# Decay attention with a mixing network: two mask buffers, masks fetched one pair ahead, later stores, fixed tiles

## The chip, the cores and the metric

The kernel runs on one core of a Trainium2 chip. The metric is the time of one execution on the device in microseconds (us), as the median of several runs. The engines are PE (matrix products), PEld (its weight loads), DVE, ACT, POOL (GpSimd) and SP, which issues nearly all DMA transfers. Each engine works through its own list of instructions in order and waits on semaphores for the others; all transfers that SP issues go through one queue.

## The reference

All tensors are fp32; B = 8 batches, H = 8 heads, S = 576 positions, D = 64.

```python
log_f  = np.log(np.clip(f, 0.0001, 1.0))
cum    = np.cumsum(log_f, axis=-1)
decay  = cum[:, :, :, None] - cum[:, :, None, :]
scores = np.where(causal, -1e9, q @ k.T / sqrt(D) + decay)   # causal: above the diagonal
attn   = softmax(scores)                                     # sum + 1e-9
x      = (attn @ v) with the 8 heads side by side            # [8, 576, 512]
h  = x.T @ U @ V                       # rank 32, mixes positions
u  = x + h.T
ch = relu(u @ w_ch1) @ w_ch2           # 512 -> 2048 -> 512
return u + ch
```

The term cum[query] is the same for a whole row of scores, so the softmax does not need it. What the kernel adds to a row of scores is -cum[key], and a very negative number above the diagonal.

## The kernel before

**The sweep.** 32 steps, one for each pair of heads (p = 0 to 31, four pairs a batch); a 33rd finishes the last pair. A step has ten slots, s = 0 to 9, of a few us each. A pair's scores are made in four row blocks of 128 positions (main blocks 0 to 3, the block i being 128(i+1) wide) and a tail of 64 positions; DVE adds the mask and takes each row's maximum (L280, tail L325), ACT exponentiates and sums (L289, L334), PE transposes the weights P in groups into PSUM tiles T (L371), and DVE and ACT copy T into PT (L356, L354). One step later, PE multiplies with the values (tile V, L413 and L415), and the result is transposed back (Tx, L428) and multiplied with the reciprocals rv of the row sums sm (L430). `inverse` makes these: two POOL operations on sm (L347, L348), DVE's reciprocal (L349), a POOL copy (L350).

**The masks.** `load_masks` (L112) builds a pair's mask in SBUF: the DMA L122 reads the row -8 cum of each of the two heads from the DRAM tensor `cumd` and broadcasts it to 128 partitions, in tiles M0 to M3 for the main blocks (128, 256, 384 and 512 KB) and M_t for the tail (two DMAs of 144 KB, L132). POOL then writes the triangle above the diagonal in place with affine_select (L124, L134). There is one buffer for each of these tiles. In step p the masks of pair p+1 are fetched: blocks 3, 1 and 0 at slot 5, block 2 and the tail at slot 7, each DMA when the tile has been read by DVE for pair p. For pair 0 the mask is a memset, and PE adds the decay.

**What else is in a step.** SP also loads q and k (`raw`, L237 to L240) two pairs ahead and v (`vr`, L252, L254) for the pair. ACT rounds q and k to the half qkh, POOL computes the rest qkl (L149, 2.8 us) for the pair after. Behind the 4th pair of each batch comes the mixing, in a step k with k mod 4 = 1 ("mixing steps" 5, 9, 13, 17, 21, 25, 29; Tu, H and `ul`, L498 to L521), which leaves u as two halves uh and ul. They are stored to the DRAM tensor `ud` (L529, L532; 1 MB each), the stores standing on SP ahead of the next step's transfers; I call the steps 10, 14, 18, 22 and 26, which begin with them, ud steps. Then the first 6 of 16 chunks of the network run as a filler of the PE (A, L565; B, L583); `ost` (L597) holds 128 rows of its sum and is stored to `accd` (L598, L602). During the first steps the network's weights are decoded (stg, L72 and L74 on POOL). After the sweep, at about 925 us, the other 10 chunks follow with Winograd-like products (pf, po, px), on weights that the loads `sr` (L800) bring.

**What sets the order.** The lists of PE and SP are in the order in which the Python code runs: each slot's calls, with `run_later` calling what `defer(phase, fn, slots)` has put off by that many slots. The lists of DVE, ACT and POOL are made by the framework's scheduler, which sorts their instructions by its own plan of times, whatever slot they were written in. SBUF for tiles is handed out by pools; a tile can be written when the space's last user is done.

## Time and profile before

| what | value |
|---|---|
| median of 3 runs | 1450.66 us (1448.24 to 1452.08) |
| profiled execution | 1444.87 us |
| its span in the trace | 1443.1 us |
| PE busy | 1224.0 us, 85% of the span |
| DVE, ACT, POOL busy | 842.5, 632.6, 265.1 us |
| instructions | 24194 |
| start of the first step, end of the sweep | 6.7 us, about 925 us |

All rows below are from the one profiled execution, which took 1444.87 us, 5.79 us less than the median. A row of a timeline is an instruction (or a few alike): start, duration, engine, line, operation with its destination and sources, and in brackets how long the engine was idle before it and who ended that. The steps begin where PE issues the scores S_0c: step 10 at 276.8 us, 12 at 340.5, 13 at 364.3, 14 at 393.4, 15 at 424.9, 19 at 535.3, 23 at 650.8, 24 at 675.7, 26 at 734.7, 30 at 851.0. Times "+x" are from the start of the step.

### The profile page before, as it was taken

To read this page: it belongs to the slowest core of one execution; us is meant where nothing else is said; L and a number is where in the kernel's file an instruction comes from. 1 tells how busy PE (TensorE), PEld (TensorE's weight loads), DVE (VectorE), ACT (ScalarE), POOL (GpSimd) and SP (SyncE) were. 2 spreads that over 40 slices of the span, in tenths; PEclk is the share of its full clock that TensorE was granted. 3 is DMA by queue.
4 is the path that set the end of the run, shared out by engine and by line. 5 is a ranking of instruction groups with operands and counts; after the bars stand their busy time and mean duration, and the time that the engine had idled before them with its cause. 6 is when DMAs were issued, how large, how long until landed. Compare 5 with 4: busy or idle time off the path is not lost.

```text
span 1443.1 us, 24194 instructions
## 1 busy us (share of the span) xinstructions
PE 1224.0 (85%) x8465; PEld 1046.7 (73%) x8465; DVE 842.5 (58%) x2151; ACT 632.6 (44%) x1675; POOL 265.1 (18%) x452
## 2 busy tenths in 40 slices
PE   6655798878878788868868877999999999999998
PEld 3432566667666667656656665798889999999998
DVE  4655644534534544534434456998387768767775
ACT  3433444433334343333433443443365555565563
POOL 2444332223223222322232222000000000000000
PEclk8766799999989899989998998999999999999999
DMA  8745564664557366354372643659467475556534
GB/s 232 169 116 116 159 127 74 174 95 97 110 141 145 73 163 121 86 164 115 81 171 66 132 151 105 216 178 310 158 218 250 149 246 192 179 186 226 167 115 121
DMA packets 152842, 219.82 MB, mean 152 GB/s; under 512 B 18000, under 2 KB 86096, under 8 KB 150672
## 3 DMA queue, kind: packets, MB, share of 16 engines
q1 hardware_dynamic: 152448, 218.01, 55.4%
q8 instruction: 67, 1.10, 0.3%
q14 instruction: 55, 0.45, 0.1%
q10 hardware_dynamic: 272, 0.26, 0.1%
HBM read 170.89 MB, written 47.33 MB: 151 GB/s over the span
## 4 chain that ended last, share of the span: by engine, by line
PE 53%; DMA 19%; DVE 5%; SPq 4%; POOL 4%; ACT 3%; issue 3%; POOLq 0%; DVEq 0%; ACTq 0%
PE pf L1083 13%; DMA M<-cumd 11%; PE po L1175 7%; PE A L565 5%; PE B L583 5%; PE px L1175 3%; DMA M_t<-cumd 3%; PE T L371 3%; PE V L413 3%; POOL qkl L149 2%; PE Hb L906 2%; PE O L922 2%; DMA ud<-ul 2%; PE pf L1175 2%; ACT P L289 2%
## 5 line engine op out<-in xcount | busy, mean ns | idle before, releaser
L371 PE MATMUL T<-ident,P 128*128 128x128 f32 x640 | 118.4, 315 | 95.1 <-DVE PT L356 86.5
L371 PEld LDWEIGHTS T<-ident,P 128*128 128x128 f32 x640 | 89.2, 163 | 117.1 <-issue 86.5
L1306 ACT COPY mc<-pf 128x512 f32<-128x512 f32 x139 | 81.6, 587 | 169.1 <-PE pf L1083 169.1
L124 POOL TENSOR_SCALAR_AFFINE_SELECT M<-M 128x256 f32<-128x256 f32 x128 | 53.4, 417 | 437.7 <-DMA M<-cumd 359.1
L565 PE MATMUL A<-uh,w1h 128*128 128x256 f32 (+1 forms) x384 | 124.0, 323 | 2.1 <-DVE hl L569 2.1
L413 PE MATMUL V<-PT,vr 128*64 128x448 f32 (+3 forms) x640 | 101.5, 459 | 26.5 <-ACT PT L354 20.9
L565 PE MATMUL A<-ul,w1h 128*128 128x256 f32 (+1 forms) x384 | 117.3, 305 | 0.0
L565 PE MATMUL A<-uh,w1l 128*128 128x256 f32 (+1 forms) x384 | 117.1, 305 | 0.0
L356 DVE COPY PT<-T 128x256 f32<-128x256 f32 (+1 forms) x192 | 73.8, 415 | 52.2 <-PE T L371 51.7
L413 PEld LDWEIGHTS V<-PT,vr 128*64 128x64 f32 x640 | 43.0, 145 | 81.1 <-issue 37.7
L1234 POOL TENSOR_TENSOR xn<-xn,xn 128x512 f32<-128x512 f32 x1 | 1.3, 1270 | 529.9 <-DMA out_dram<-xn 529.9
L583 PE MATMUL B<-w2h,hh 128*128 128x512 f32 x216 | 94.7, 438 | 3.3 <-DVE ost L597 3.3
L349 DVE RECIPROCAL rv<-sm 128x9 f32<-128x9 f32 x32 | 6.9, 214 | 144.1 <-POOL sm L348 144.1
L583 PE MATMUL B<-w2l,hh 128*128 128x512 f32 x216 | 88.3, 409 | 0.0
L583 PE MATMUL B<-w2h,hl 128*128 128x512 f32 x216 | 87.9, 407 | 0.0
L565 PEld LDWEIGHTS A<-uh,w1h 128*128 128x128 f32 x384 | 76.9, 200 | 2.8 <-DVE hl L569 2.3
L569 DVE SCALAR_TENSOR_TENSOR hl<-A,hh 128x256 fp32r<-128x256 f32 (+1 forms) x96 | 43.3, 452 | 59.0 <-ACT hh L573 59.0
L565 PEld LDWEIGHTS A<-uh,w1l 128*128 128x128 f32 x384 | 76.9, 200 | 0.1
L565 PEld LDWEIGHTS A<-ul,w1h 128*128 128x128 f32 x384 | 76.5, 199 | 0.2 <-DVE ul L503 0.2
L149 POOL TENSOR_TENSOR qkl<-raw,qkh 128x1216 fp32r<-128x1216 f32 x26 | 72.4, 2783 | 15.2 <-ACT qkh L146 14.2
L1083 PE MATMUL pf<-d,b1h 128*128 128x256 f32 x320 | 69.5, 280 | 0.0
L446 ACT CAST xh<-xn 128x640 fp32r<-128x640 f32 x32 | 23.2, 726 | 102.7 <-DVE xn L395 102.7
(321 smaller groups left out, 3909.7 us busy)
## 6 DMA issues: line engine op xcount, KB each, us to landing
un<-ud SPq DMA_DIRECT2D x16, 1024.0 KB, 6.4
M<-cumd SPq DMA_DIRECT2D x31, 512.0 KB, 5.7
d<-ud SPq DMA_DIRECT2D x48, 256.0 KB, 4.2
M<-cumd SPq DMA_DIRECT2D x31, 384.0 KB, 5.9
twd<-xn SPq DMA_DIRECT2D x40, 256.0 KB, 2.9
raw<-in_qk_dram SPq DMA_DIRECT2D x32, 288.0 KB, 8.2
Th<-twd SPq DMA_DIRECT2D x35, 256.0 KB, 3.7
tw<-twd SPq DMA_DIRECT2D x35, 256.0 KB, 2.9
```

Of the source, the lines that this page charges most:

```text
L124: nc.gpsimd.affine_select(d, d, [[0, 2], [-1, P]], ALU.is_ge, MASKED, base=0, channel_multiplier=1)
L149: leng.tensor_tensor(dl, src, dh.bitcast(F32), op=ALU.subtract)
L289: nc.scalar.activation(pt, ps, AF.Exp, bias=z["nm"][:, col : col + 1], scale=-1.0, accum_out=z["sm"][:, col : col + 1])
L356: defer(2, lambda: nc.vector.tensor_copy(dst, src))
L371: nc.tensor.transpose(tp[:, P * (x + c) : P * (x + c) + P], z["P"][j][i][:, P * c : P * c + P], ident)
L413: nc.tensor.matmul(ps, vr[:, c, j], pt[:, j, c, lo:hi], start=c == 0, stop=lo == 0)
L565: nc.tensor.matmul(ps[:, :nt], wt[:, fc, c], ut[:, c, sl], start=m == 0, stop=m == 3 * NDC - 1)
L569: nc.vector.scalar_tensor_tensor(hl[:, fc, :nt], ps[:, :nt], 0.0, hh.bitcast(F32)[:, fc, :nt], op0=ALU.max, op1=ALU.subtract)
L583: nc.tensor.matmul(ps, ht[:, fc, P * x : P * x + P], wt[:, fc], start=fc == 0 and m == 0, stop=fc == NA - 1 and m == 2,)
L1083: nc.tensor.matmul(ps, a[x][:, c], b[y][:, c], start=start and m == 0, stop=m == 5, skip_group_check=True)
L1175: nc.tensor.matmul(ps[:, HT * x : HT * x + HT], f[a][:, P * x : P * x + P], w[b], start=k.i == 0 and m == 0 and x == 0 and not (k.n == NG ...
L1306: nc.scalar.copy(mc, FA)
```

## The change

Masks get two buffers (pool `sb2` for `sb`). In step p the masks of pair p+2 are fetched, all five tiles at slot 5, ahead of q and k in the code. The triangles become a function of their own, `triangles`, called for pair p+1 at slot 4 (blocks 3, 1, 0) and at slot 7 (block 2 and tail). The masks of pair 1 are fetched at the start, right behind the store of `cumd`. The `ud` stores are put off by 5 slots for 2, the `accd` stores by 3 slots where they followed at once. The tiles for v are two fixed ones whose empty half is zeroed once, so one of three DMAs for each pair goes; the tile PT4 is one fixed tile, zeroed once, so the memset L365 in each step goes.

```diff
--- before.py
+++ after.py
@@ -104,35 +104,46 @@
     nc.vector.memset(warm, 1.0)
     for raw in RAW:
         nc.vector.memset(raw[:, QT:KO], 0.0)
+    VR = [att.tile([P, NM + 1, P], F32, name=f"vr{x}") for x in range(2)]
+    for vr in VR:
+        nc.gpsimd.memset(vr[64:128, NM], 0.0)
+    PT4 = att.tile([P, P], F32, name="PT4")
+    nc.gpsimd.memset(PT4[64:128], 0.0)
     ident = cst.tile([P, P], F32, name="ident")
     make_identity(nc, ident)
     xn = [cst.tile([P, NM + 1, DM], F32, name=f"xn{i}") for i in range(NX)]
 
-    def load_masks(p, mains):
+    def load_masks(p):
         if p >= NP:
             return
-        z = st[p]
-        for i in (3, 1, 0) if mains == 0 else (2,):
+        z = st.setdefault(p, {"M": {}})
+        for i in (3, 1, 0, 2):
             w = P * (i + 1)
-            m = z["M"][i] = sb.tile([P, 2, w], F32, tag=f"M{i}", name=f"M{p}_{i}")
+            m = z["M"][i] = sb2.tile([P, 2, w], F32, tag=f"M{i}", name=f"M{p}_{i}")
             if p == 0:
                 nc.gpsimd.memset(m, 0.0)
             else:
                 src = cumd.rearrange("(j p) s -> p j s", j=2)[p, :, 0:w]
                 nc.sync.dma_start(m, src.unsqueeze(0).broadcast_to([P, 2, w]))
-            d = m[:, :, P * i : w]
-            nc.gpsimd.affine_select(d, d, [[0, 2], [-1, P]], ALU.is_ge, MASKED, base=0, channel_multiplier=1)
-        if mains == 0:
-            return
-        m = z["M"][NM] = sb.tile([P, S], F32, tag="Mt", name=f"M{p}_t")
+        m = z["M"][NM] = sb2.tile([P, S], F32, tag="Mt", name=f"M{p}_t")
         if p == 0:
             nc.gpsimd.memset(m, 0.0)
+            return
         for j in range(2):
-            if p:
-                nc.sync.dma_start(m[OWN[j]], cumd[j * B * NHP + p].unsqueeze(0).broadcast_to([64, S]))
-            d = m[OWN[j], MAIN:S]
-            nc.gpsimd.affine_select(d, d, [[-1, TAIL]], ALU.is_ge, MASKED, base=0, channel_multiplier=1)
-
+            nc.sync.dma_start(m[OWN[j]], cumd[j * B * NHP + p].unsqueeze(0).broadcast_to([64, S]))
+
+    def triangles(p, rows):
+        if p >= NP:
+            return
+        for i in rows:
+            m = st[p]["M"][i]
+            if i < NM:
+                d = m[:, :, P * i : P * i + P]
+                nc.gpsimd.affine_select(d, d, [[0, 2], [-1, P]], ALU.is_ge, MASKED, base=0, channel_multiplier=1)
+                continue
+            for j in range(2):
+                d = m[OWN[j], MAIN:S]
+                nc.gpsimd.affine_select(d, d, [[-1, TAIL]], ALU.is_ge, MASKED, base=0, channel_multiplier=1)
 
     w1h = wt.tile([P, NA, NDC, P], F32R, name="w1h")
     w1l = wt.tile([P, NA, NDC, P], F32R, name="w1l")
@@ -233,7 +244,7 @@
             return
         b, hp = divmod(p, NHP)
         raw = RAW[p % 2]
-        st[p] = {"b": b, "hp": hp, "raw": raw, "M": {}}
+        st.setdefault(p, {"M": {}}).update(b=b, hp=hp, raw=raw)
         nc.sync.dma_start(raw[:, KO:QW], qk[p, :, 1])
         nc.sync.dma_start(raw[:, 0:MAIN], qk[p, :, 0, 0:MAIN])
         for j in range(2):
@@ -247,11 +258,10 @@
 
     def load_v(p):
 
-        vr = sb2.tile([P, NM + 1, P], F32, tag="vr", name=f"vr{p}")
+        vr = VR[p % 2]
         st[p]["vr"] = vr.rearrange("p c (j d) -> p c j d", j=2)
         nc.sync.dma_start(vr[:, 0:NM], v[p, 0:MAIN].rearrange("(c p) d -> p c d", p=P))
-        for r in range(2):
-            nc.sync.dma_start(vr[64 * r : 64 * r + 64, NM], v[p, MAIN:S])
+        nc.sync.dma_start(vr[0:64, NM], v[p, MAIN:S])
 
     def terms(p):
         z = st[p]
@@ -361,8 +371,6 @@
         z = st[p]
         if "PT" not in z:
             z["PT"] = sb.tile([P, 2, NM, S], F32, tag="PT", name=f"PT{p}")
-            z["PT4"] = sb.tile([P, P], F32, tag="PT4", name=f"PT4{p}")
-            nc.gpsimd.memset(z["PT4"][64:128], 0.0)
         tp = psT.tile([P, 512], F32, tag="T", name=f"T{p}_{j}{g}")
         x = 0
         for i in GRP[g]:
@@ -383,8 +391,7 @@
     def turn_keys(p):
         tq = psT.tile([P, 512], F32, tag="T", name=f"Ty{p}")
         nc.tensor.transpose(tq[0:64, 0:P], st[p]["ptl"][:, MAIN:S], ident)
-        pt4 = st[p]["PT4"]
-        defer(0, lambda: nc.scalar.copy(pt4[0:64], tq[0:64, 0:P]))
+        defer(0, lambda: nc.scalar.copy(PT4[0:64], tq[0:64, 0:P]))
 
     def turn_last(p):
         z = st[p]
@@ -413,7 +420,7 @@
                 nc.tensor.matmul(ps, vr[:, c, j], pt[:, j, c, lo:hi], start=c == 0, stop=lo == 0)
         for j in range(2):
             nc.tensor.matmul(
-                rest[OWN[j], MAIN - P : S - P], vr[:, NM, j], z["PT4"][:, 64 * j : 64 * j + 64], start=False, stop=True
+                rest[OWN[j], MAIN - P : S - P], vr[:, NM, j], PT4[:, 64 * j : 64 * j + 64], start=False, stop=True
             )
         defer(1, lambda: nc.vector.tensor_copy(xT[:, 0:P], head[:, 0:P]))
         defer(1, lambda: nc.vector.tensor_copy(xT[:, P:S], rest[:, 0 : S - P]))
@@ -531,7 +538,7 @@
                         jt = b // 2
                         nc.sync.dma_start(ud[B, :, x, :, P * jt : P * jt + P], t.bitcast(F32)[:, :, MAIN : MAIN + P])
 
-            defer(4, use, 2)
+            defer(4, use, 5)
 
         h = [(0.43, lambda i=i: hmix(i)) for i in range(NM + 1)]
         t = [(0.43, lambda i=i: tu(i)) for i in range(NM)] + [(0.25, tv)]
@@ -595,11 +602,11 @@
                     ost = sf2.tile([P, DM], F32, tag="ost", name=f"ost{b}_{ci}")
                     if ci < NM:
                         nc.vector.tensor_tensor(ost, ps, X[:, ci], op=ALU.add)
-                        nc.sync.dma_start(accd[b, ci], ost)
+                        defer(5, lambda: nc.sync.dma_start(accd[b, ci], ost), 3)
                     else:
                         nc.vector.tensor_tensor(ost[0:64], ps[0:64], X[0:64, NM], op=ALU.add)
                         nc.vector.tensor_tensor(ost[64:128], ps[64:128], xn[(b - 1) % NX][0:64, NM], op=ALU.add)
-                        nc.sync.dma_start(accd[B, b // 2], ost)
+                        defer(5, lambda: nc.sync.dma_start(accd[B, b // 2], ost), 3)
 
                 defer(1, use)
 
@@ -639,13 +646,14 @@
         ):
             own = ident[rows, col : col + 1]
             nc.vector.tensor_scalar(picks[rows, cols], warm[rows, cols], own, -8.0, op0=ALU.mult, op1=ALU.mult)
-        load_masks(0, 0)
+        load_masks(0)
+        triangles(0, range(NM + 1))
         nc.vector.tensor_tensor_scan(fr, fl, fl, 0.0, op0=ALU.add, op1=ALU.bypass)
-        load_masks(0, 1)
         load_qk(1)
         load_w(1)
         nc.vector.tensor_scalar(fl[0 : B * H], fr[0 : B * H], -8.0, None, op0=ALU.mult)
         nc.sync.dma_start(cumd, fl[0 : B * H])
+        load_masks(1)
         load_v(0)
         for i in range(NX - 1):
             nc.gpsimd.memset(xn[i][64:128, NM, :], 0.0)
@@ -716,15 +724,17 @@
                 stay_awake(1)
             if s == 4 and ps_ and p:
                 load_v(p)
-            if s == 5 and ps_:
-                load_masks(p + 1, 0)
+            if s == 4 and ps_:
+                triangles(p + 1, (3, 1, 0))
             if s == 6 and ps_:
                 load_qk(p + 2)
                 if p == 0:
                     load_w(2)
                     load_w(3)
+            if s == 5 and ps_:
+                load_masks(p + 2)
             if s == 7 and ps_:
-                load_masks(p + 1, 1)
+                triangles(p + 1, (2, NM))
 
             if ps_ and s == 0:
                 run_a(p)
@@ -851,7 +861,7 @@
                 if wb[0] == (2, 1):
                     weight_sums(0)
                 wb_unit(*wb.pop(0))
-        for _ in range(3):
+        for _ in range(6):
             run_later()
     for x in wb:
         wb_unit(*x)
```

On POOL, in step 14. M15 and M16 are the masks of pairs 15 and 16, qkl15 the rest of q and k of pair 15, sm14 and rv14 the row sums of pair 14, xl13 a half of pair 13's result. Before:

```order
L365 MEMSET PT414_3903 64x128
L124 AFFINE_SELECT M15_3_3930<-M15_3_3930 128x2x128
L124 AFFINE_SELECT M15_1_3935<-M15_1_3935 128x2x128
L124 AFFINE_SELECT M15_0_3940<-M15_0_3940 128x256
L149 TENSOR_TENSOR qkl15_3927<-raw1_89,qkh15_3926 128x1216
L347 TENSOR_TENSOR sm14_3744<-sm14_3744 128x1
L124 AFFINE_SELECT M15_2_3991<-M15_2_3991 128x2x128
L134 AFFINE_SELECT M15_t_3996<-M15_t_3996 64x64 x2
L348 TENSOR_SCALAR sm14_3744<-sm14_3744 128x9
L350 COPY rv14_4098<-rv14_4098 64x1
L447 TENSOR_TENSOR xl13_3987<-xn0_99,xh13_3986 128x512
```

and after the change:

```order
L142 AFFINE_SELECT M16_3_3896<-M16_3_3896 128x2x128
L142 AFFINE_SELECT M16_1_3898<-M16_1_3898 128x2x128
L142 AFFINE_SELECT M16_0_3900<-M16_0_3900 128x256
L160 TENSOR_TENSOR qkl15_3893<-raw1_89,qkh15_3892 128x1216
L142 AFFINE_SELECT M16_2_3902<-M16_2_3902 128x2x128
L146 AFFINE_SELECT M16_t_3904<-M16_t_3904 64x64
L357 TENSOR_TENSOR sm14_3705<-sm14_3705 128x1
L146 AFFINE_SELECT M16_t_3904<-M16_t_3904 64x64
L358 TENSOR_SCALAR sm14_3705<-sm14_3705 128x9
L360 COPY rv14_4055<-rv14_4055 64x1
L454 TENSOR_TENSOR xl13_3949<-xn0_105,xh13_3948 128x512
```

The triangles of pair 16 stand in step 14, where those of pair 15 stood; the triangle of block 2 and one of the tail's now stand ahead of the first operation on sm14; the memset is gone. In the steps 6 to 29 this order repeats (in the mixing steps the tail's triangles stand between the two operations on sm). Before, 12 of these 24 steps had block 2 and the tail behind both operations on sm (9, 11, 12, 13, 15, 17, 20, 21, 23, 25, 28, 29), and steps 19 and 27 all five tiles; step 30, which had pair 31's masks behind them, now has none.

On SP, from step 13's transfers to step 14's (accd and ud are the stores, raw q and k, vr the values). Before:

```order
L598 DMA accd<-ost1_3_3654 128x512
L237 DMA raw1_89<-in_qk_dram 128x576
L238 DMA raw1_89<-in_qk_dram 128x512
L240 DMA raw1_89<-in_qk_dram 64x64 x2
L122 DMA M14_2_3684<-cumd 128x2x384
L132 DMA M14_t_3689<-cumd 64x576 x2
L529 DMA ud<-uh2_3640 128x4x512
L529 DMA ud<-ul2_3641 128x4x512
L252 DMA vr14_3898<-in_v_dram 128x4x128
L254 DMA vr14_3898<-in_v_dram 64x128 x2
L122 DMA M15_3_3930<-cumd 128x2x512
L122 DMA M15_1_3935<-cumd 128x2x256
```

and after the change:

```order
L127 DMA M15_2_3591<-cumd 128x2x384
L133 DMA M15_t_3593<-cumd 64x576 x2
L248 DMA raw1_89<-in_qk_dram 128x576
L249 DMA raw1_89<-in_qk_dram 128x512
L251 DMA raw1_89<-in_qk_dram 64x64 x2
L605 DMA accd<-ost1_3_3620 128x512
L536 DMA ud<-uh2_3606 128x4x512
L536 DMA ud<-ul2_3607 128x4x512
L263 DMA vr0_94<-in_v_dram 128x4x128
L264 DMA vr0_94<-in_v_dram 64x128
L127 DMA M16_3_3896<-cumd 128x2x512
L127 DMA M16_1_3898<-cumd 128x2x256
```

Block 2, the tail and raw are ahead of the accd store, and M16 is fetched in step 14 where M15 was. Elsewhere on SP: of the accd stores that stood ahead of vr and the masks, those of steps 15 and 23 now stand behind the masks, those of the mixing steps stay ahead, and step 19 and 27 have one ahead of the masks (stored from an ost made at about +4.4) for two.

On POOL, in the first steps (stg0 and stg1 are weights to be decoded, w1l their lower half). Before:

```order
L347 TENSOR_TENSOR sm0_190<-sm0_190 128x1
L348 TENSOR_SCALAR sm0_190<-sm0_190 128x9
L350 COPY rv0_382<-rv0_382 64x1
L124 AFFINE_SELECT M1_2_307<-M1_2_307 128x2x128
L134 AFFINE_SELECT M1_t_312<-M1_t_312 64x64
L72 TENSOR_TENSOR stg0_133<-stg0_133 128x512
L134 AFFINE_SELECT M1_t_312<-M1_t_312 64x64
L124 AFFINE_SELECT M2_3_458<-M2_3_458 128x2x128
L74 TENSOR_TENSOR w1l_103<-stg0_133,w1h_102 128x512
L124 AFFINE_SELECT M2_1_463<-M2_1_463 128x2x128
L124 AFFINE_SELECT M2_0_468<-M2_0_468 128x256
L72 TENSOR_TENSOR stg1_176<-stg1_176 128x512
```

and after the change:

```order
L357 TENSOR_TENSOR sm0_205<-sm0_205 128x1
L358 TENSOR_SCALAR sm0_205<-sm0_205 128x9
L142 AFFINE_SELECT M2_3_282<-M2_3_282 128x2x128
L360 COPY rv0_395<-rv0_395 64x1
L142 AFFINE_SELECT M2_1_284<-M2_1_284 128x2x128
L142 AFFINE_SELECT M2_0_286<-M2_0_286 128x256
L142 AFFINE_SELECT M2_2_288<-M2_2_288 128x2x128
L146 AFFINE_SELECT M2_t_290<-M2_t_290 64x64 x2
L72 TENSOR_TENSOR stg0_139<-stg0_139 128x512
L142 AFFINE_SELECT M3_3_476<-M3_3_476 128x2x128
L74 TENSOR_TENSOR w1l_109<-stg0_139,w1h_108 128x512
L142 AFFINE_SELECT M3_1_478<-M3_1_478 128x2x128
```

The decoding of stg0 stands behind all masks of pair 2 for those of pair 1; that of stg1 (row behind the last) stands behind blocks 3, 1 and 0 of pair 3. Besides: in the mixing steps DVE's first `ul` stands ahead of the reciprocal rv, behind which it stood before; and three of the `sr` loads, which SP issued in the first 20 us, follow after the sweep, since the second mask buffer takes the space they had.

## Rows read from the trace of the kernel before

**Rows 1.** Windows: length, busy time by engine, PE clock, DMA share, GB/s.
```profile
147.10:925.00 777.90, 627.09 (x4266) 508.83 (x4266) 372.94 (x1106) 308.44 (x898) 200.57 (x350) 0.90 0.51 122
925.00:1443.10 518.10, 510.92 (x3790) 487.87 (x3788) 387.51 (x832) 266.89 (x619) 1.27 (x1) 0.99 0.60 195
```

**Rows 2.** Waits, 150 to 880 us: us in total, times, longest.
```profile
POOL M L124 <- DMA M<-cumd: 299.9, 81, 15.5
...
DVE rv L349 <- POOL sm L348: 127.0, 22, 11.9
...
PE T L371 <- DVE PT L356: 71.0, 15, 11.6
...
PE Tu L512 <- DVE ul L503: 37.0, 7, 6.3
```

**Rows 3.** Timeline, POOL, step 14: start, us, operation, idle before.
```profile
415.60 0.41 POOL L124 TENSOR_SCALAR_AFFINE_SELECT M<-M 128x256 f32<-128x256 f32 x1 [0.70 <-DMA M<-cumd]
...
416.92 0.25 POOL L348 TENSOR_SCALAR sm<-sm 128x9 f32<-128x9 f32 x1
```

**Rows 4.** Timeline, DVE, step 14.
```profile
417.21 0.22 DVE L349 RECIPROCAL rv<-sm 128x9 f32<-128x9 f32 x1 [8.16 <-POOL sm L348]
```

**Rows 5.** Timeline, PE: its stop in ud step 10 (first of five).
```profile
302.80 0.45 PE L371 MATMUL T<-ident,P 128*128 128x128 f32 x1 [7.72 <-DVE PT L356]
```

**Rows 6.** The same in step 26 (last of five).
```profile
762.73 1.51 PE L371 MATMUL T<-ident,P 128*128 128x128 f32 x6 [9.79 <-DVE PT L356]
```

**Rows 7.** Windows: 7 us behind step 14's stop.
```profile
418.00:425.00 7.00, 6.95 (x38) 6.45 (x40) 2.77 (x8) 1.62 (x4) 1.73 (x2) 0.64 0.00 0
```

**Rows 8.** Timeline, SP, step 30: one pair's masks in one piece.
```profile
870.02 2.41 SPq L122 DMA_DIRECT2D M<-cumd  x4
```

**Rows 9.** Timeline, POOL, step 30: the last triangle of these masks.
```profile
886.13 0.24 POOL L134 TENSOR_SCALAR_AFFINE_SELECT M_t<-M_t 64x64 f32<-64x64 f32 x1 [0.27 <-DMA M_t<-cumd]
```

**Rows 10.** DMA issues from 393.9 us on: KB, us to landing.
```profile
ud<-uh SPq DMA_DIRECT2D x1, 1024.0 KB, 6.8
```

**Rows 11.** The same from 167.5 us on (step 5, queue empty).
```profile
ud<-uh SPq DMA_DIRECT2D x1, 1024.0 KB, 4.3
```

**Rows 12.** Timeline, SP, step 14: issue, length, transfer.
```profile
399.65 2.42 SPq L122 DMA_DIRECT2D M<-cumd  x3
```

**Rows 13.** The same, step 12.
```profile
343.04 1.65 SPq L122 DMA_DIRECT2D M<-cumd  x3
```

**Rows 14.** Timeline, POOL, step 23.
```profile
672.17 0.25 POOL L348 TENSOR_SCALAR sm<-sm 128x9 f32<-128x9 f32 x1
```

**Rows 15.** Timeline, PE: its stop in step 15 (first of four).
```profile
447.31 0.87 PE L371 MATMUL T<-ident,P 128*128 128x128 f32 x3 [3.83 <-DVE PT L356]
```

**Rows 16.** The same in step 28 (last of four).
```profile
815.22 1.17 PE L371 MATMUL T<-ident,P 128*128 128x128 f32 x6 [3.45 <-DVE PT L356]
```

**Rows 17.** Timeline, SP, step 19.
```profile
539.66 0.33 SPq L598 DMA_DIRECT2D accd<-ost  x1
```

**Rows 18.** Timeline, POOL, step 19.
```profile
550.06 0.24 POOL L348 TENSOR_SCALAR sm<-sm 128x9 f32<-128x9 f32 x1
```

**Rows 19.** Timeline, PE, step 13 (a mixing step).
```profile
387.68 1.11 PE L512 MATMUL Tu<-ident,xn 128*128 128x128 f32 x4 [5.20 <-DVE ul L503]
```

**Rows 20.** Timeline, SP, first 45 us.
```profile
11.89 0.38 SPq L122 DMA_DIRECT2D M<-cumd  x1
...
14.62 3.43 SPq L800 DMA_DIRECT2D sr<-in_w_dram  x3
```

**Rows 21.** Timeline, POOL, first 60 us.
```profile
35.71 1.27 POOL L72 TENSOR_TENSOR stg<-stg 128x512 f32<-128x512 f32 x1
...
42.28 1.84 POOL L72 TENSOR_TENSOR stg<-stg 128x512 f32<-128x512 f32 x2
```

**Rows 22.** Timeline, ACT, first 60 us.
```profile
37.01 0.62 ACT L73 CAST w1h<-stg 128x512 fp32r<-128x512 f32 x1 [7.72 <-POOL stg L72]
```

**Rows 23.** Timeline, PE, first 60 us.
```profile
38.72 5.39 PE L413 MATMUL V<-PT,vr 128*64 128x128 f32 x20 [5.75 <-ACT PT L354]
```

## The prediction

> **What bounds the kernel now.** I read the windows by stage first. Behind 925 us PE is busy 510.9 of 518.1 us, so nothing of this change can shorten that stretch; from 147 to 925 us, 27 of the 32 steps, it is busy 627.1 of 777.9 us at a mean granted clock of 0.90 [rows 1]. So 150.8 us of PE idleness and some lost clock lie in the steps that the change touches. The waits of that stretch come second: the reader is to see one chain in four rows [rows 2]. POOL's triangles wait 299.9 us for mask transfers, DVE's reciprocal rv waits 127.0 us for POOL's sm, PE's transposes T wait 71.0 us for DVE's copies PT and its Tu 37.0 us for ul. PE's 108.0 us are the end of that chain, and the mask transfer its beginning; POOL's own 299.9 us cost only what they pass on.
>
> The timelines of one step show the links. In step 14 the triangle of block 2 (415.60 us, 0.70 us of waiting for its transfer) and the tail's stand ahead of the second operation on sm (416.92) [rows 3]; rv, next on DVE, starts at 417.21 after 8.16 us of waiting for it [rows 4]; PT stands behind rv, and PE behind PT. The stop takes 7.72 us in the first and 9.79 us in the last of the five ud steps [rows 5, 6]. Behind a stop the clock is at its lower level for a while: in the 7 us that follow step 14's, PE is busy 6.95 us, but the mean clock is 0.64 [rows 7], so of the two levels (1.2 and 2.4 GHz) most of that time had the lower. That loses 0.36 x 7 = 2.5 us beside the stop.
>
> So the question is when sm comes. It does not wait for the pair's own masks, but for masks that were issued in the same step and that nothing needs before the next.
>
> **The change part by part.**
>
> *Masks a pair further ahead.* From the words of the change one would expect the wait to go: a transfer a whole step old has landed. But POOL's list is made by the scheduler, and its place for the triangles of pair p+2 is step p, right behind the issue. The waiter has moved with the transfer. So the first term is zero, and what counts is when the last triangle of a step's masks can run. Step 30 of before shows the price of one pair's five tiles in one piece: issued from 870.02 us, last triangle done at 886.13 + 0.24 = 886.37 [rows 8, 9], 16.35 us; with sm's 0.25 us [rows 3] it is 16.6 us from the first mask's issue to sm. That is my rule for every step of the changed kernel: sm comes 16.6 us after SP issues block 3.
>
> The Trainium skill's page "DMA: Bandwidth & Descriptors", section "Bandwidth", has a measured 1 MB transfer at 6.15 us; by it the 1.57 MB of a pair would be in after some 9.5 us, an estimate. The trace has 16.35 us for them, and I use that.
>
> *Where block 3 is issued.* Four classes of steps.
>
> Ud steps (10, 14, 18, 22, 26). The two stores of 1 MB stay ahead of the masks, but raw, block 2 and the tail of the mixing step before are no longer in the queue ahead of the stores, since accd no longer holds them up on SP. The first store now takes 6.8 us to land [rows 10]; with an empty queue, in step 5, it took 4.3 us [rows 11]. Masks and sm come 2.5 us earlier: 5 x 2.5 = 12.5 us gained (0, if SP's issue at 399.65 us [rows 12] sets the time and not the queue, to 20 us with the vr transfer saved).
>
> Ordinary steps 15, 23, 24, 28. Where block 3 is issued early, as in step 12 at 343.04 - 340.5 = +2.5 us [rows 13], the rule gives sm at +19.1. Steps 15 and 23 get there because accd now stands behind the masks. Step 23 had sm at 672.42 - 650.8 = +21.6 [rows 14]; that is 2.5 us. PE stopped 3.83 us in the first and 3.45 us in the last of these four [rows 15, 16], so the stops shrink to about 1.2 us: 4 x 2.5 = 10 us. Of the clock's 2.5 us I give back half in each, as a short stop may cost no clock: 4 x 1.25 = 5 us at most, of which I take 3.
>
> Steps 19 and 27. Here SP had come late with the masks and POOL had put them behind sm, which was done at 550.30 - 535.3 = +15.0 [rows 18], with no stop of PE. Now accd goes at 539.66 [rows 17], +4.4, block 3 at +4.8, sm is behind it, at +21.4. PE arrives there at about +18.6 (447.31 - 3.83 - 424.9 in step 15 [rows 15]) and goes on some 0.9 us after sm: a new stop of 3.7 us, with the clock 6.2 us; twice, 12.4 us lost. Steps 11, 12, 16 and 20 stay as they are by the rule, to 1.5 us each either way.
>
> Mixing steps (six of this kind from 9 on). One accd store, waiting for its ost, stays ahead of the masks, and one vr transfer less brings block 3 from +7.0 to +6.4; sm comes at +23.0. PE's stop in step 13 ended at 387.68 - 364.3 = +23.4 with a Tu group of 1.11 us next [rows 19]. The first ul stands ahead of rv now, so that group runs before the stop, and the T behind it at +23.9: 1.1 - 0.5 = 0.6 us gained in each, 3.6 us. The same order on DVE with less time in the queue could make it 2 us each; block 2 and the tail, now ahead of sm, -2 us each.
>
> Sum of the steps: 12.5 + 10 + 3 - 12.4 + 3.6 = 16.7 us gained.
>
> *The first steps.* Pair 1's masks still wait for cumd, so the first goes at about 11.9 us as now [rows 20]. But the decoding of the first weights, 35.71 us [rows 21], stood behind pair 1's masks alone, and now stands behind pair 2's as well; ACT's cast waits for it (7.72 us [rows 22]), PT's copy stands behind the cast, and PE's V at 38.72 us [rows 23] behind that. Two pieces of 16 us from 11.9 us on end at 44 us, 8 us late. Against that, three sr loads (issued over 3.43 us [rows 20]) and a vr leave this stretch; with the queue never empty the pieces may follow each other faster. The second decoding, at 42.28 us [rows 21], stands behind blocks of pair 3. I take 5 us lost, between 12 lost and 3 gained.
>
> *The sr loads* come after the sweep, with decodings that DVE and ACT did earlier. DVE has 518.1 - 387.5 = 130.6 us free there [rows 1], but at the start less: 3 us lost, between 0 and 10.
>
> *The rest.* The memset L365 and the second vr tail lie in POOL's and SP's waits, so they are worth nothing by themselves. The later accd stores read ost tiles that are rewritten later; if one held DVE up, it would be 1 to 2 us in a step.
>
> Sum: 16.7 - 5 - 3 = 8.7 us gained. The profiled execution took 1444.87 us, so 1436.2; the median lies 5.8 us higher, so 1442.
>
> **The rivals.**
>
> *Nothing net.* The ud steps are bound by SP's issue and not by the queue, so their 12.5 us stay out. For it: in step 14 block 3 is issued 6.3 us into the step [rows 12], and that may be most of the delay. Against it: the store's landing time shows a queue that was not empty. Then 16.7 - 12.5 - 8 = 3.8 us lost on the profiled execution, less what the clock may give: 1447 to 1455, say 1452.
>
> *Slower: the row sums wait longer than before.* In 12 steps block 2 and the tail stood behind sm, and in two all tiles; now none. If a piece takes 18 us and not 16.35, because raw shares the queue or the tail's DMA waits for DVE's reading of the tail, sm comes 1.65 us later in all 24 steps, and PE stops that much longer: 40 us against the 16.7 gained. Half of it, as not all steps have PE waiting, and the first steps at 8 us lost: 16.7 - 20 - 8 - 3 = 14.3 us lost, 1465. It decides from about 17 us for a piece.
>
> *The masks go off the path.* If the transfers landed before qkl is done, the 71.0 + 37.0 us of stops and most of the clock behind 22 of them (22 x 2.5 = 55) would go: 1450.7 - 108 - 40 = about 1303; half of that 1375. For it: block 2 and the tail are issued some 7 us earlier in a step than in step 14 (behind block 0 and not behind raw). Against it: the order on POOL and the 16.35 us. The Trainium skill, same page, section "Rules for kernel authors", says to issue a transfer early and wait for it late; the change does the first half only, so the rule speaks against a gain here.
>
> **How the numbers follow.** The forecast has 0.47, nothing net 0.20, slower 0.26, off the path 0.07. What a measurement of this kernel can tell from no change is 0.3%, 4.4 us: below 1446.3 or above 1455.0. Faster is the forecast and the last rival less a little of the forecast's upper end, 0.52; same 0.21; slower 0.27. The unknowns (ud 0 to 20, steps 19 and 27, the mixing steps 12 either way, the start -12 to 3, sr 0 to -10) give the forecast's own range, 1420 to 1456. The range goes to 1465 for the slower rival, and to 1405 for part of the third.
>
> **What would show it.** In the profile after: POOL's triangles still waiting about 300 us, with sm behind them in every step from 6 to 29; sm at about +19 in ordinary steps, +21 in 19 and 27, +23 in mixing and ud steps; Tu's 37.0 us small and T's wait larger, together 90 to 105 us; the first ud store landing in under 5.5 us; PE's first long V at 41 to 46 us; the sum from 147 to 925 us shorter by some 17 us. Wrong would be: triangles that run without waiting, stops of PE that end before the last mask lands, or a first step that begins earlier.

## The result: 0.6% slower

| | before | after |
|---|---|---|
| median of 20 runs each, same chip | 1450.92 us | 1459.38 us |
| range of the runs | 1445.71 to 1454.61 | 1451.03 to 1464.63 |
| profiled execution (span) | 1444.87 (1443.1) us | 1459.31 (1457.5) us |

The ratio of after to before is 1.0058 [1.0044, 1.0072]: 8.5 us slower, where 1442 us, 8.7 us faster, was forecast. The profiled execution of before lies 6 us below its median and that of after on it, so the two traces differ by 14.4 us. That is the difference that the views below share out.

The windows come first, cut where step 5 and where step 31 begin. Of after (length, busy time of PE, PEld, DVE, ACT and POOL with instructions, PE clock, DMA share, GB/s):

```profile
6.70:155.80 149.10, 80.63 (x400) 48.67 (x399) 78.51 (x208) 53.84 (x156) 58.60 (x87) 0.70 0.66 151
155.80:901.50 745.70, 591.48 (x4020) 482.10 (x4019) 344.70 (x1033) 290.37 (x850) 188.89 (x311) 0.90 0.51 118
901.50:1457.50 556.00, 543.90 (x4038) 513.81 (x4037) 415.07 (x904) 285.10 (x666) 4.28 (x7) 1.00 0.59 192
```

The same of before:

```profile
6.70:147.10 140.40, 80.70 (x402) 48.37 (x401) 78.92 (x210) 54.62 (x156) 57.56 (x84) 0.69 0.66 160
147.10:878.50 731.40, 591.02 (x4018) 480.50 (x4017) 340.36 (x1026) 289.43 (x848) 195.76 (x339) 0.90 0.52 121
878.50:1443.10 564.60, 546.99 (x4038) 516.21 (x4037) 420.09 (x911) 285.91 (x668) 6.08 (x13) 0.99 0.58 190
```

The first steps are 8.7 us longer, steps 5 to 30 14.3 us longer, and all that follows 8.6 us shorter. In the middle stretch PE is busy equally long, at the same clock of 0.90. What grew there is idleness of PE, from 140.4 to 154.2 us. The waits of after, 150 to 890 us since that stretch is longer (us in total, times, longest), answer to [rows 2]:

```profile
POOL M L142 <- DMA M<-cumd: 426.2, 90, 18.0
...
DVE rv L359 <- POOL sm L358: 152.4, 25, 12.5
...
PE T L379 <- DVE PT L366: 125.5, 23, 10.7
```

The chain has the same links, each of them longer, and Tu's 37.0 us have become 2.8 us in a single wait. T and Tu together wait 128.3 us, where they waited 108.0. Masks fetched a pair earlier have therefore not shortened any wait for them.

By kind of step, with the length of all steps of the kind together and means in us from the step's start ("block 3" is when SP issues the first mask of the step):

| steps | length of all, before, after | block 3, before, after | sm, before, after | sm as predicted |
|---|---|---|---|---|
| mixing 9, 13, ... 29 | 174.8, 184.0 | +7.1, +6.4 | +22.5, +24.3 | +23 |
| ud 10, 14, ... 26 | 163.7, 167.3 | +7.6, +5.1 | +25.5, +25.8 | +23 |
| 11, 15, 19, 23, 27 | 133.0, 133.7 | -, +3.8 | +18.7, +21.1 | +19, +21 in 19 and 27 |
| 12, 16, 20, 24, 28 | 132.4, 132.4 | -, +2.6 | +19.7, +20.0 | +19 |

So block 3 went out as early as forecast, in the ud steps 2.5 us earlier to the digit, and sm still came no earlier. Step 14 of after shows why. SP's queue (start, us, operation):

```profile
406.06 0.38 SPq L536 DMA_DIRECT2D ud<-uh  x1
407.27 0.37 SPq L536 DMA_DIRECT2D ud<-ul  x1
...
410.50 7.49 SPq L127 DMA_DIRECT2D M<-cumd  x4
418.77 4.31 SPq L133 DMA_DIRECT2D M_t<-cumd  x2
```

POOL in the same step, with the idle time before an instruction and its releaser in brackets:

```profile
429.80 0.41 POOL L142 TENSOR_SCALAR_AFFINE_SELECT M<-M 128x256 f32<-128x256 f32 x1 [0.84 <-DMA M<-cumd]
431.14 0.23 POOL L146 TENSOR_SCALAR_AFFINE_SELECT M_t<-M_t 64x64 f32<-64x64 f32 x1 [0.93 <-DMA M_t<-cumd]
...
431.93 0.25 POOL L358 TENSOR_SCALAR sm<-sm 128x9 f32<-128x9 f32 x1
```

And PE:

```profile
433.05 1.52 PE L379 MATMUL T<-ident,P 128*128 128x128 f32 x6 [9.27 <-DVE PT L366]
```

Block 3 is issued at 410.50 and sm is done at 432.18: 21.7 us, and not 16.6. PE stops for 9.27 us, where it stopped for 7.86 in step 14 before. The two stores of 1 MB lie in the queue ahead of the masks. In step 14 block 3 itself landed at +11.9 (before +13.8), but from there to the last tile it took 12.4 us (before 9.3). So only 1.9 us of the earlier issue reached the head, the end came later, and POOL waits for the end. In an ordinary step the forecast's rule nearly holds. SP and POOL in step 12:

```profile
354.87 9.14 SPq L127 DMA_DIRECT2D M<-cumd  x4
```

```profile
371.58 0.25 POOL L358 TENSOR_SCALAR sm<-sm 128x9 f32<-128x9 f32 x1
```

That is 16.96 us from the issue to the end of sm. From the issue to the last tile's landing the means are 16.6 us (steps 12 to 28) and 16.5 us (11 to 27) in the ordinary steps, 17.3 in the mixing steps and 20.0 in the ud steps.

That the rule nearly holds there is in part luck. The two buffers hold the masks of pairs p and p+1, so those of pair p+2 go into the tiles of pair p, which DVE still reads in step p. In step 12 SP sends blocks 3, 1 and 0 within 1.3 us and block 2 only at 363.65 us, 0.1 us after DVE has read the old block 2; step 30 of before, which gave the rule, had no such wait.

A mixing step of after, 13, on DVE:

```profile
394.27 0.69 DVE L510 TENSOR_TENSOR ul<-Tu,uh 128x512 fp32r<-128x512 f32 x1 [0.36 <-ACT uh L509]
400.74 0.21 DVE L359 RECIPROCAL rv<-sm 128x9 f32<-128x9 f32 x1 [5.78 <-POOL sm L358]
```

PE's T behind them:

```profile
402.19 0.88 PE L379 MATMUL T<-ident,P 128*128 128x128 f32 x3 [6.31 <-DVE PT L366]
```

As predicted, ul runs ahead of rv, and the Tu group that stopped for 5.20 us [rows 19] does not wait any more. But the T behind it waits 6.31 us for the same sm.

In the first steps POOL's second decoding, which answers to [rows 21], and the cast that waits for the first:

```profile
48.28 0.41 POOL L142 TENSOR_SCALAR_AFFINE_SELECT M<-M 128x256 f32<-128x256 f32 x1 [5.50 <-DMA M<-cumd]
...
52.35 1.76 POOL L72 TENSOR_TENSOR stg<-stg 128x512 f32<-128x512 f32 x2
```

```profile
42.81 0.62 ACT L73 CAST w1h<-stg 128x512 fp32r<-128x512 f32 x1 [10.37 <-POOL stg L72]
...
53.66 0.62 ACT L73 CAST w1h<-stg 128x512 fp32r<-128x512 f32 x1 [8.70 <-POOL stg L72]
```

The first cast comes 5.80 us later than in [rows 22], and PE's first long V at 44.52 us, 5.80 us later than in [rows 23]. Step 2 begins 6.4 us later than before (63.2 for 56.9), and steps 2 to 4 add 2.4.

What became shorter lies in step 31, which the prediction had not read by itself. Before, SP issued pair 31's masks in step 30 [rows 8], and two stores of decoded weights (wd) behind them. ACT's cast of step 31 waited for these stores, PT's copy stood behind the cast, and PE's V waited for the copy. SP, ACT and PE of before:

```profile
875.55 5.75 SPq L671 DMA_DIRECT2D wd<-xn  x2
```

```profile
886.60 0.62 ACT L73 CAST xn<-xn 128x512 fp32r<-128x512 f32 x1 [8.89 <-DMA wd<-xn]
888.46 0.58 ACT L354 COPY PT<-T_t 128x512 f32<-128x512 f32 x1
```

```profile
889.10 0.69 PE L413 MATMUL V<-PT,vr 128*64 128x128 f32 x4 [5.52 <-ACT PT L354]
891.40 3.91 PE L413 MATMUL V<-PT,vr 128*64 128x448 f32 x16 [1.61 <-ACT PT L387]
```

After, step 30 loads no masks (pair 31's went in step 29), and PE's long V of step 31 runs at 906.43 without a stop:

```profile
906.43 3.12 PE L420 MATMUL V<-PT,vr 128*64 128x128 f32 x20
```

### The profile page after: what moved, and what is told of

The parts are those of the page before. It is cut to its first block, busy times and chain, and to the rows that moved or that the text cites. A ratio compares the mean times of both kernels' runs of the same rounds, so it can differ in the third digit from the quotient of the medians.

```text
span 1457.5 us, 24048 instructions
## 1 busy us (share of the span) xinstructions
PE 1221.3 (84%) x8465; PEld 1046.2 (72%) x8465; DVE 841.4 (58%) x2151; ACT 632.5 (43%) x1675; POOL 257.8 (18%) x423
## 4 chain that ended last, share of the span: by engine, by line
PE 54%; DMA 25%; DVE 9%; issue 4%; ACT 4%; POOL 3%; SPq 1%; POOLq 0%; DVEq 0%; ACTq 0%
DMA M_t<-cumd 16%; PE pf L1093 13%; PE po L1185 7%; PE A L572 5%; PE B L590 5%; DMA M<-cumd 4%; PE V L420 4%; PE px L1185 3%; PE T L379 3%; ACT P L299 2%; PE pf L1185 2%; PE Tt L470 2%; PE Hb L916 2%; PE S_0c L278 1%; PE po L1200 1%
## 5 line engine op out<-in xcount | busy, mean ns | idle before, releaser
L453 ACT CAST xh<-xn 128x640 fp32r<-128x640 f32 x32 | 23.2, 726 | 161.7 <-DVE xn L402 161.7
```

## The experiments

All ratios are against the kernel before on the same chip, with a 95% interval. That kernel's median was 1457.8 to 1460.3 us there, so the times in us that the expectations name, which start from 1451 and 1459, are to be read as ratios. The theory under test is the one chain: masks issued in a step, POOL's triangles of that same step that wait for them, sm behind these triangles, rv, PT, PE. The rivals are that the sums are not what PE waits for, that the pace of the transfers is set by what is ahead of them or by themselves, and that one half of the change alone brings the loss.

**1 and 2: the two operations on sm on DVE**, in the kernel after and in the kernel before. This takes sm out from behind the triangles and leaves all else.

```diff
-        nc.gpsimd.tensor_tensor(sm[:, 8:9], sm[:, 8:9], sm[:, 9:10], op=ALU.add)
-        nc.gpsimd.tensor_scalar(sm[:, 0:9], sm[:, 0:9], 1e-9, None, op0=ALU.add)
+        nc.vector.tensor_tensor(sm[:, 8:9], sm[:, 8:9], sm[:, 9:10], op=ALU.add)
+        nc.vector.tensor_scalar(sm[:, 0:9], sm[:, 0:9], 1e-9, None, op0=ALU.add)
```

> The kernel after the change, with the two small operations on the row sums sm moved from POOL to DVE, ahead of the reciprocal there. Theory A (the row sums stand behind the triangles of masks that were issued in the same step, and PE's stops at T come from that alone): rv waits for no mask any more, T's waits of 125.5 us in 23 stops between 150 and 890 us fall below 30 us, and the time falls by 60 to 110 us, to 1350 to 1400 us. Theory B (POOL's lower halves xl, which stand behind the same triangles, hold the PE next, at Tt): most stops stay as stops at Tt, and the time is 1425 to 1445 us. Theory C (the masks' landing does not matter, DVE or the queue does): within 5 us of 1459.

> The kernel before the change, with the same two operations on DVE. Theory A: the stops at T and Tu (108.0 us) go, 1345 to 1390 us. Theory B: 1415 to 1440 us, less held up than the changed kernel, since xl stands ahead of block 2 and the tail in about half of the steps. Theory C: within 5 us of 1451.

Measured: 0.9578 [0.9553, 0.9604] for after and 0.9598 [0.9573, 0.9623] for before. Waits of the first, 150 to 840 us:

```profile
POOL M L142 <- DMA M<-cumd: 360.7, 77, 18.0
...
PE Tt L470 <- POOL xl L454: 75.5, 22, 7.9
```

T's stops fell from 125.5 to 10.0 us, so sm behind the triangles was their cause. But the next product of POOL that PE needs, xl, stands behind the same triangles, and PE now waits 75.5 us for that (63.2 us in the second kernel). So theory A holds for T's stops and theory B for what came in their place. Once sm is off POOL the two kernels are level within their intervals, and steps 5 to 30 take 685.5 and 684.3 us, where they took 745.7 and 731.4: the change's loss in the steps comes through sm.

**3 and 4: the change in its two halves**: the masks alone (two buffers, fetched a step ahead, triangles in other slots; the three sr loads then come after the sweep), and the rest alone (stores and fixed places; the sr loads stay early).

```diff
 # 3, against before
-        for i in (3, 1, 0) if mains == 0 else (2,):
-            m = z["M"][i] = sb.tile([P, 2, w], F32, tag=f"M{i}", name=f"M{p}_{i}")
+        for i in (3, 1, 0, 2):
+            m = z["M"][i] = sb2.tile([P, 2, w], F32, tag=f"M{i}", name=f"M{p}_{i}")
...
 # 4, against before
-            defer(4, use, 2)
+            defer(4, use, 5)
...
-                        nc.sync.dma_start(accd[b, ci], ost)
+                        defer(5, lambda: nc.sync.dma_start(accd[b, ci], ost), 3)
```

> Only the part on the masks: two buffers, one pair further ahead, triangles as their own function; stores, tiles for v and PT4 as before the change. Theory A (the masks' part places block 2 and the tail ahead of the row sums in every step, and that is the loss): 1456 to 1466 us, ud and mixing steps with sm as late as in the changed kernel. Rival (the later stores do it, as they fall into the masks' time): 1440 to 1450 us.

> Only the other parts: ud and accd stores later, fixed tiles for v and PT4; one mask buffer, fetched for the next pair as before. The scheduler here puts block 2 and one triangle of the tail ahead of the row sums too, as in the changed kernel, though raw stands between on SP. Theory A (the place on POOL decides): slower than before, 1453 to 1465 us. Rival (the masks' part alone makes the loss): 1440 to 1450 us.

Measured: the masks alone 1.0229 [1.0197, 1.0260], the rest alone 1.0020 [1.0002, 1.0039], both together 1.0058. They do not add up. Each half alone makes steps 5 to 30 longer, 766.4 and 765.7 us for 731.4, where both together take 745.7, so neither rival holds, and the masks alone lose more than their theory named. In both, sm comes later than before: +24.1 and +24.7 us for +22.5 in the mixing steps, +21.1 and +23.3 for +18.7 in steps 11 to 27. With the masks alone, accd stays ahead of them: block 3 goes out at +8.0, +4.0, +8.8 and +9.2 in steps 15, 20, 23 and 28, and sm comes at +23 to +27. Why the two together lose less is not shown further. In the first steps the halves do add up: step 5 starts at 163.5 with the masks alone and at 139.0 with the rest alone, against 147.1 before, +16.4 and -8.1, and 155.8 in after. From step 31 on, the rest alone, with the sr loads early, takes 553.2 us and after 556.0; but kernel 5 below, whose sr loads come as late as in after, takes 553.6. So no price of the late loads shows.

**5, 6 and 7: POOL in the order of the code.** The scheduler places POOL's instructions; in these kernels POOL joins PE and SP in the part that keeps the order as written, from step 8 on (5, and 7 on the kernel before) or from the start (6).

```diff
-    with tc.manual_schedule(engines={ET.PE, ET.SP}):
+    with tc.manual_schedule(engines={ET.PE, ET.SP, ET.Pool}):
         for t in range(8, LAST + 1):
```

> The kernel after the change, with POOL's list too in the order in which the code is written, from step 8 on, so that the triangles of pair p+1 run in step p, on masks that were fetched in step p-1, and sm, rv and xl stand ahead of them. Theory A (what the scheduler makes of POOL's order took the gain away): POOL's waits for masks fall from 426 us to under 60 us, the stops at T (125.5 us) and those at Tt that came in their place with the sums on DVE (75.5 us) fall below 40 us together, the ratio to the kernel before is 0.92 to 0.95. Rival (the masks' transfers hold PE by another way, the queue or DVE): 0.96 to 1.00.

> The same from step 0 on: the decoding of the weights no longer stands behind all masks of pair 2. Theory A: step 5 begins at 140 to 148 us (155.8 in the changed kernel, 147.1 before), 6 to 16 us less than with the order from step 8 on. Rival (the queue, full in the first 60 us, delays the weights): step 5 within 4 us of 155.8, and the time equal within 5 us.

> The kernel before the change, with POOL's list in the order of the code from step 8 on: xl stands behind the triangles of blocks 3, 1 and 0 of the next pair, fetched in the same step, and sm behind those of block 2 and the tail. Theory A (two buffers are worth something once POOL's order is as written): POOL still waits over 200 us for masks, PE stops at Tt, ratio 0.95 to 0.98, at least 1.5% above the changed kernel with the same order. Rival (the order alone is the gain, and the second buffer is worth nothing): within 1% of it.

Measured: 0.8997 [0.8974, 0.9020], 0.8863 [0.8840, 0.8886] and 0.9611 [0.9559, 0.9664]. In kernels 5 and 6 the triangles now stand where the code has them, a step behind their transfer, and run almost without waiting. Kernel 5 on POOL, at the end of step 14 and the start of step 15:

```profile
389.55 0.25 POOL L358 TENSOR_SCALAR sm<-sm 128x9 f32<-128x9 f32 x1
390.11 0.18 POOL L360 COPY rv<-rv 64x1 f32<-64x1 f32 x1 [0.31 <-DVE rv L359]
390.37 1.12 POOL L142 TENSOR_SCALAR_AFFINE_SELECT M<-M 128x256 f32<-128x256 f32 x3
```

sm stands ahead of the next three triangles, and these follow one another in 1.12 us. But the order on POOL is not all that changed. sm is done at +22.2 us in step 14, no earlier than in an ordinary step of after, and PE does not stop for it, because the scheduler has also moved rv on DVE. Kernel 5 on DVE:

```profile
387.95 0.56 DVE L366 COPY PT<-T 128x384 f32<-128x384 f32 x1 [1.13 <-PE T L379]
...
389.83 0.21 DVE L359 RECIPROCAL rv<-sm 128x9 f32<-128x9 f32 x1 [0.41 <-POOL sm L358]
```

In after, four to six of the step's copies PT on DVE stand behind rv in steps 9 to 29 and wait with it; in kernel 5 at most one does. So three links went at once: the triangles' wait, rv ahead of PT, and xl behind the triangles. These runs do not tell their shares apart.

Kernel 6 by windows, cut at steps 5 and 31:

```profile
6.70:142.30 135.60, 78.38 (x400) 47.16 (x399) 80.52 (x207) 54.88 (x156) 53.87 (x75) 0.70 0.73 163
142.30:736.40 594.10, 553.64 (x4018) 446.50 (x4017) 344.42 (x1033) 290.28 (x850) 192.86 (x323) 0.99 0.67 149
```

Step 5 begins at 142.3 us, 16.0 us earlier than in kernel 5 (158.3), as theory A said: the decoding behind all masks of pair 2 was the loss of the first steps. Steps 5 to 30 take 594.1 us instead of 745.7. PE is busy 553.64 us where it was 591.48, for as many matmuls, and the granted clock of the stretch rose from 0.90 to 0.99 as the stops went. 151.6 us are gained there, 113.8 of them idleness and 37.8 clock. The expectation for kernel 5, 0.92 to 0.95, had been too small. In kernel 6 the largest wait on POOL is now for ACT's qkh:

```profile
POOL qkl L160 <- ACT qkh L157: 221.1, 21, 14.2
```

These 221.1 us do not reach PE, which stops for qkl nowhere in that stretch; its T waits 9.6 us in all, and the triangles wait 1.5 us for masks. Kernel 7 shows what the whole change is worth with POOL as written: with one buffer, POOL still waits for masks, though less than the 200 us that the expectation named. Its waits, 150 to 845 us:

```profile
POOL M L124 <- DMA M<-cumd: 159.5, 50, 8.3
...
DVE rv L349 <- POOL sm L348: 67.6, 23, 5.2
```

PE stops there for Tt (28.5 us, for POOL's xl) and for V (34.8 us, for the copy into PT4). The order alone gives 3.9%, the order with the change 10.0%. The change is worth 6.4% (0.8997 / 0.9611) where the waiter stands a step behind the transfer. That is the worth of the whole change and not of the second buffer alone: the memset of PT4, which the change takes out, waits 187.7 us on POOL in kernel 7, ahead of what follows it in the list. Kernel 6, at 1294.53 us, takes 11% less than before.

**8: the loads of raw later**, so that nothing lies between the masks: slot 9 instead of 6 from step 8 on.

```diff
-            if s == 6 and ps_:
+            if s == (9 if p and p > 7 else 6) and ps_:
```

> The kernel after the change, with the q and k loads (raw) at slot 9 for slot 6 from step 8 on, POOL's order unchanged. Theory A1 (the masks of a pair take 18.4 us and not 16.4 from the first issue to the row sums, because raw follows them closely in the queue): sm comes 1 to 2 us earlier in most steps, the time falls by 15 to 30 us, ratio 0.985 to 0.995. Rival A2 (the masks set their own pace, whatever follows): sm within 0.5 us of the changed kernel's in ordinary steps, ratio 1.00 to 1.01.

Measured: 1.0012 [0.9987, 1.0037], against after's 1.0058. Issue to last landing is 16.9, 16.4, 20.3 and 16.5 us (steps 12 to 28, mixing, ud, 11 to 27), where it was 16.6, 17.3, 20.0 and 16.5. Only the mixing steps gain, 0.9 us in the piece and 4.1 us in the six steps together. So raw behind the masks does not set their pace in the other steps, and it is not what made the ud piece long.

**9 and 10: the stores behind the masks**: the ud stores 11 slots on instead of 5, and, in a kernel of its own, the accd stores 6 slots on instead of 3.

```diff
 # 9
-            defer(4, use, 5)
+            defer(4, use, 11)
 # 10
-                        defer(5, lambda: nc.sync.dma_start(accd[b, ci], ost), 3)
+                        defer(5, lambda: nc.sync.dma_start(accd[b, ci], ost), 6)
```

> The kernel after the change, with the ud stores put off by 11 slots for 5, so that in steps 10, 14, 18, 22 and 26 they stand behind the masks and raw. The failed step of the prediction was that the masks of these steps land 2.5 us earlier than before. Theory B1 (the two stores of 1 MB ahead of the masks are what delays sm there): block 3 is issued at about +2.5, sm comes at +19 to +21 for +23.8 to +28.0, PE's stops in the five steps fall from 45.7 us together to 5 to 20 us, the time falls by 25 to 45 us. Rival B2 (the masks are late there for another reason, such as the vr load or DVE's reading): sm stays at +23 or later, time within 8 us.

> The kernel after the change, with the accd stores put off by 6 slots for 3, so that in the mixing steps the store that waits for its ost stands behind the masks; POOL's order unchanged. Theory A (sm comes one piece, 16.5 to 18 us, after block 3 is issued, and the waiting store is what holds block 3 back to +6.4 there): block 3 at +2.5 to +3.5 in steps 9, 13, 17, 21, 25, 29, sm at +20 to +21.5 for +24.3, PE's stops in these steps fall from 43.9 us together to under 25, the time falls by 15 to 40 us. Rival (the mixing steps hold sm by something else, DVE's ul or POOL's wait for DVE): sm stays above +23, time within 8 us.

Measured: 0.9909 [0.9876, 0.9942] and 0.9819 [0.9789, 0.9849]. Kernel 9 in step 14, on SP and POOL:

```profile
408.55 8.35 SPq L127 DMA_DIRECT2D M<-cumd  x4
...
424.49 0.53 SPq L536 DMA_DIRECT2D ud<-uh  x1
```

```profile
427.70 0.25 POOL L358 TENSOR_SCALAR sm<-sm 128x9 f32<-128x9 f32 x1
```

sm is done 19.4 us behind block 3's issue and not 21.7, and in the mean of the ud steps at +21.3 instead of +25.8, since block 3 also goes out at +2.5 instead of +5.1. The stops of PE's T there fall from 45.6 to 23.0 us, and the five steps together from 167.3 to 142.1. Against after's 1.0058 that is 1.5%, some 22 us. All three numbers fall a little short of theory B1's, but the rival B2 is out. Kernel 10 in step 13:

```profile
379.40 9.70 SPq L127 DMA_DIRECT2D M<-cumd  x4
...
393.94 0.58 SPq L605 DMA_DIRECT2D accd<-ost  x1
```

```profile
396.89 0.25 POOL L358 TENSOR_SCALAR sm<-sm 128x9 f32<-128x9 f32 x1
```

Here the piece stays at 17.3 us and only its start moves, from +6.4 to +2.6. sm moves with it, from +24.3 to +20.6, and the stops of PE's T in the mixing steps fall from 44.0 to 21.2 us, all within theory A. So the two stores act in different ways: the ud stores take time in the queue, and an accd store that waits for its ost holds SP's issue.

## Why the prediction was wrong

**The chain and the moved waiter: right.** The waiter did move with the transfer, so the term for masks a pair ahead is zero. It is less than that, because POOL's triangles of all blocks now stand ahead of sm. Kernels 1 and 2 show it: with sm off POOL, the steps of the two kernels are level.

**The ud steps: the step that failed.** The prediction said "Masks and sm come 2.5 us earlier: 5 x 2.5 = 12.5 us gained". The head did: block 3 was issued at +5.1 for +7.6 and landed at +12.7 for +14.9 (means of the five), and the first ud store of step 14 took 4.2 us to land, for 6.8 [rows 10]. The end did not follow. From block 3's landing to the last tile's it took 12.4 us for 10.7. And sm came 0.7 us behind that last landing in all five steps, where before it had come ahead of it in three of them (10, 18, 26). So sm stayed where it was (+25.8 for +25.5), and the five steps lost 3.6 us: 16 us from the forecast. The rule of 16.6 us could not have warned of it, as it came from step 30 [rows 8, 9], where nothing of 2 MB stood ahead of the masks; in the ud steps sm came 17.9 us behind block 3's issue already before, and 20.7 us after.

Kernel 9, with the stores behind the masks, gets 17.9 us from the issue to the last landing and 25 us of shorter steps, so the stores ahead are what keeps sm late in these steps. They act on the head: without them block 3 lands 5.7 us after its issue and not 7.5. The stretch behind it stays at 12.2 us in kernel 9, so what made it longer than the 10.7 us of before is not the stores, and stays open.

**The mixing steps: sign wrong.** 3.6 us gained were forecast, with -2 us each named as the other end. The Tu group did go ahead, but 17.3 us for the piece and block 2 and the tail ahead of sm brought sm to +24.3 and cost 9.2 us over six steps, 1.5 us in each.

**Ordinary steps: the sum right, not each step.** By the rule sm was due at +19.1 and came at +20.0 in steps 12 to 28. Step 15 fell from 26.3 to 22.8 us and 23 from 24.8 to 22.3, 6.0 us together. Step 27 rose from 23.2 to 29.3, as forecast (6.2); step 19, forecast to lose as much, fell from 27.4 to 26.7. Steps 11 to 28 of these two kinds together lost 0.7 us, where 0.6 us gained (10 + 3 - 12.4) was forecast. That the sums agree so well is luck.

**The slower rival came true at its own condition.** It "decides from about 17 us for a piece". From block 3's issue to the last landing the mean over the 21 steps of the four kinds is 17.6 us. Of its two reasons, raw in the queue is out for the ud steps by kernel 8. The other, the tail's DMA waiting for DVE's reading, is seen in every step (in step 12 block 2 and the tail go out 0.1 us after DVE's reads), but in the ud steps it did not decide: in step 14 block 2 was issued at +10.6, 8.1 us before block 0 had landed.

**The first steps** lost 8.7 us, for 5 with bounds of -12 and 3; PE's first V at 44.52 us lies in the forecast's 41 to 46. **The sr loads:** 3 us were taken for them; the runs show none (kernels 4 and 5 differ by 0.4 us from step 31 on). **Missed:** the 7.1 us of V's stops in step 31 of before. Both were in the trace, at 889 and 891 us, in the stretch up to 925 us that the prediction read as one. After has no mask ahead of the wd stores in step 30 and no such stop; kernel 2, which keeps before's order there, stops for 6.5 and 1.6 us. This gain was luck: without it after would be 7.1 us slower still.

T and Tu together waited 128.3 us where 90 to 105 was named as the sign of the forecast, and POOL 426.2 us for masks where 300 was: both point to the slower rival.

Left open: why a pair's masks need 16 us in step 30 with almost nothing ahead of them; no kernel here loaded them in another form.

## What to carry to other kernels

Here a transfer issued a step earlier paid only where the instruction that waits for it did not move with it. Where a scheduler places that instruction, look where it ended up: the same change cost 0.6% as placed and gained 6.4% with POOL in the order written. When one engine's list is fixed, look at the other engines' lists too, since the scheduler may move their instructions as well, as it did with rv. When a queue's start moves, work out the end of the whole piece in each kind of step, with what is ahead of it there, and not its head.

## What the runs showed of the hardware

The masks are slow without filling the DMA engines. Before, in step 30, where their 1.57 MB were almost alone, the windows end like this (columns as in the first windows):

```profile
875.00:878.00 3.00, 3.00 (x23) 2.51 (x22) 2.91 (x7) 0.51 (x2) 2.17 (x3) 1.00 0.47 73
878.00:881.50 3.50, 3.50 (x30) 2.77 (x29) 2.91 (x7) 0.00 (x0) 0.60 (x1) 1.00 0.23 64
```

At 64 GB/s the DMA engines are busy 0.23 of the time, while tiles are still to come: the triangle at 886.13 waits for one [rows 9]. Blocks 1, 0 and 2 (256, 128 and 384 KB) land 3.2, 3.1 and 3.2 us one behind another, so there it is not their size that sets the time. Each has 256 packets, which begin over some 4.3 us, and most packets take 25 to 84 ns. So what is short is not the engines' time; what it is, the runs don't show.

With the stops of T at 9.6 us in all (kernel 6), steps 5 to 30 ran at a mean granted clock of 0.99 for 0.90, and PE was busy 37.8 us less for as many matmuls. The prediction's rival had put 2.5 us of clock to each of 22 stops and counted 40 us of them, close to that.
